# An output sum in a PSUM tile of its own, a new program order, single transfers, and weights split earlier, in a convolution with a gated feed-forward layer

## The chip, the cores and the metric

The kernel runs on one core of a Trainium2 chip. A core has a matrix engine (TensorE, PE in the profile, with its weight loads PEld), a vector engine (VectorE, DVE), an activation engine (ScalarE, ACT), GpSimd (POOL) and a queue that issues transfers (SyncE, SP). Each works through its own instructions in order and waits for the others by semaphores; 16 DMA engines carry the transfers. SBUF is the working memory, PSUM the accumulators that TensorE writes. The metric is the time of one execution in microseconds (us), as the median of several runs.

## What is computed

A causal convolution of 7 taps, one softmaxed set of taps for each of 8 heads, over x of shape (8, 4096, 192), then a feed-forward layer on the 32768 rows:

```python
w = softmax(weight)                      # (8, 7)
out[b, s, h, g] = sum_k w[h, k] * x_pad[b, s + k, h, g]
x = out.reshape(32768, 192)
xn = x / sqrt(mean(x * x) + 1e-6) * rms_g
g = xn @ w_gate                          # (192, 1536)
val = xn @ w_val
result = (silu(g) * val) @ w_out         # (1536, 192)
```

## The kernel before

**Tiles.** Rows go in pairs of two tiles of 512 (`T`), 1024 rows (`PT`) a pair, 32 pairs. The depth 192 is folded as 3 x 64, and gate and value products run side by side on the two halves of TensorE's rows (64 each). The hidden width 1536 is 12 blocks of 128, taken as 6 groups `j` of two blocks.

**The normal pair (2 to 31).** Both products are done with the seven-product scheme for a 2 x 2 block product. One factor is the pair's x in quarters, the other the weights. For exactness in the fast 32-bit format, each operand is split into three parts, so one product is 3 parts x 2 halves = 6 matmuls (line 936). A group `j` has 11 products, P1 to P7 and Q1 to Q4, into four blocks a, b, c, d, each a two-bank PSUM tile (one half gate, one half value): 66 products a pair. Between products the blocks are combined: `f1` copies a to b (ACT), `f3` copies c out (ACT), `f4` and `f5` add into c and d (DVE, line 1005). When a block is ready, `ga` to `gd` take the silu of its gate half (ACT, line 1011) and `ma` to `md` multiply its value half by that (DVE, line 1018); both give the PSUM tile back. The output product uses the scheme too: h sums `h1` to `h4` (POOL, line 988), then 42 output steps `o1.k` to `o7.k` of 12 matmuls (line 961) into three sums X, Y, Z, with `c1` (copy X to Y, ACT), `s7` and `c2` (copies of Z and X, ACT), `C21`, `C22` (DVE, line 1035) and the transposes `T11` to `T22` (DVE, line 976) into an output tile, which `st0` and `st1` store.

**PSUM.** Eight banks are four tiles of two banks (`duo`). A pool `pool4` hands them out in the order in which they came back. X and Z are the two halves of one of them (`"XZ"`), Y has one.

**Ahead of a pair.** For a later pair: `ld` (x loads by head), `cv0` to `cv6` (the taps; 0 on ACT, the others DVE line 437), `sq`, `red`, `pow`, `bc`, `mul` (the norm; `mul` is POOL line 516), `pl` (puts the result away in DRAM by heads), `ft` (fetches it back transposed into `rb`, line 662), `x1` to `x5` (sums of x quarters, line 862), and per group of operands `k`, `n`, `l`, `d` (the split; lines 835, 698, 843, 845).

**The weights.** `prepare` computes for each of 9 weight combinations the three split parts on POOL, DVE and ACT (lines 767 to 782) and stores them to DRAM (`wd`, line 786). It has 50 steps. From there a ring of 12 slots in SBUF is refilled while the pairs run (`ring_load`, line 804, 54 pieces a pair): a slot's next load is issued where its last product stands in the program, and SP waits there until TensorE has done it. `ring_start` issues the first 12.

**The order** is written out as words. `ORDER` is one normal pair, run for each pair, `FIRST` is pair 1, and `LINE` is the order of the products and output steps on TensorE. A word is an engine letter (V: DVE, A: ACT, G: POOL, S: SP), an operation and an index; `+` means that it works for a pair ahead, `-` for the pair before; `p3` issues the next three entries of `LINE`; `W` is one step of `prepare`, `R` is `ring_start`. Words of one engine run in the order written.

**The start.** Pair 0 and pair 1 use plain products (lines 1119 and 907) with unsplit weights. Pair 0's output phase (line 1160) is laid out on a time scale: every item is `put` at a place and emitted in the order of places; `base` is where the phase begins and its 96 steps are 37.5 units apart. Its sums leave PSUM by an ACT copy (line 1168) and a DVE addition (line 1172). Pair 1's products follow, 24 in thirds (72 steps, line 907), then its output steps. In `FIRST` the 50 `W` stand between pair 1's products, and `R` after them; the fetch of pair 2, `Sft.0+` to `Sft.2+`, comes after `R`. The taps of pair 2 run beside pair 0's output phase, cut in three pieces of 512 columns that accumulate in PSUM (`part_tap`, lines 453 and 461).

Of the kernel before, what the change touches and what calls it, by code (L numbers as in the profile page):

```python
# [11 lines left out]
F32 = mybir.dt.float32  # L12
# [8 lines left out]
def kernel(  # L21
# [28 lines left out]
    Q = 32  # L50
# [19 lines left out]
    HIGH = 0xFFFFF000  # L70
    PLAIN = tuple((j, c) for j in range(NP) for c in "abcd")
    ORDER = (
        "VT21- p2 Af1.0 p3 Af3.0 Spl.0+ Gh4.0- p1- Vf4.0 p1 Acv0++ p2 Aga.0 p1 p1- Spl.1+",
        "Gh4.3- Vma.0 Gh4.2- p1- Vf5.0 p1 Vcv1++ p1 Agc.0 Agb.0 Vmc.0 p1 Gh4.1- Gh4.4- Vmb.0",
        "Agd.0 Sst1- p2 Vmd.0 Spl.2+ Spl.3+ Af1.1 Sft.0+ p1 Vcv2++ Af3.1 p1 p2- Vf4.1 p1- p2",
        "Agc.1 p2 Vcv3++ VT12- Aga.1 Vmc.1 p1 Vf5.1 Gh1.0 p1 Gh3.0 Sft.2+ Agd.1 Vma.1 Sft.1+",
        "Vmd.1 p2 Af1.2 p3 Vcv4++ p1 Af3.2 Aga.2 Vf4.2 p2 Vma.2 Agb.1 p1 Vmb.1 Vf5.2 p2 Agc.2",
        "p1 Vmc.2 Agd.2 p2 Vmd.2 Vcv5++ Gh1.1 Af1.3 p1 Gx1+ Af3.3 p2 Vf4.3 p1 Agb.2 Vmb.2",
        "Gh1.2 Aga.3 Vma.3 p3 Agc.3 Vf5.3 Vmc.3 p2 Agd.3 Vmd.3 p1 Af1.4 p2 Gx3+ p1 Af3.4",
        "Vcv6++ Gx5+ Gh3.1 Agb.3 p1 Vf4.4 Gh3.2 p1 Aga.4 Vmb.3 p2 Agc.4 p1 Vma.4 Vf5.4 p1",  # L80
        "Sld.0+++ Vmc.4 Agb.4 p1 Agd.4 Gh1.3 p1 Vmb.4 p2 Vmd.4 Af1.5 Sld.1+++ p1 Af3.5 p2",
        "Gx2+ p1 Gx4+ p1 Gh1.4 Vk.3+ p1 Vd.3+ p1 Gh2.0 Vf4.5 An.3+ p1 Gh3.3 p2 Vl.3+ Aga.5 p1",
        "Vk.0+ p1 Gh3.4 Vma.5 Asq++ Agc.5 Gh2.1 Vf5.5 p1 Vd.0+ Vmc.5 An.0+ p1 Agd.5 Sld.2+++",
        "Ac1 Gh2.4 p1 Vmd.5 Gh2.3 Agb.5 p2 Sld.3+++ Gh2.2 p1 Vmb.5 Gh1.5 p1 Sld.4+++ Vred++",
        "p1 Sld.5+++ p1 Gh3.5 p4 Vl.0+ Sld.6+++ Gh2.5 As7 Vk.1+ p1 Vd.1+ p2 An.1+ Vl.1+ p2",
        "Vk.2+ Sst0- Gpow++ p2 Vl.2+ Vd.2+ p2 Ac2 p1 An.2+ p2 Vbc++ Vk.4+ p1 Sld.7+++ An.4+",
        "VT11 p1 VC21 Gh4.5 p1 Vd.4+ Vl.4+ p2 Gmul++ p1 VC22 VT22",
    )
# [1291 lines left out]
```

## Time and profile before

| | us |
|---|---|
| median of 3 runs | 2845.02 (2844.59 to 2846.81) |
| the profiled execution: its time | 2841.62 |
| the profiled execution: its span | 2839.7 |
| first matmul of pair 1 (line 907) | 134.7 |
| first matmul of pair 2 (line 936) | 274.5 |
| from pair 2 to pair 3 | 94.7 |
| from one pair to the next, pairs 3 to 30 | 84.1 to 87.6 |
| first matmul of pair 31 | 2747.3 |

Costs of single instructions, from the groups by line (mean ns, and how many):

```profile
L1005 DVE TENSOR_TENSOR ps<-ps,tt 128x1024 f32<-128x1024 f32 x360 | 443.5, 1232 | 216.8 <-PE ps L936 113.4
L1018 DVE TENSOR_TENSOR ht<-ps,tt 128x512 f32<-128x512 f32 x744 | 510.8, 688 | 255.0 <-ACT tt L1011 240.7
L437 DVE SCALAR_TENSOR_TENSOR y<-xh,tp,y 128x1536 f32<-128x1536 f32 x180 | 344.8, 1916 | 0.0
L862 POOL TENSOR_TENSOR tt<-xb 128x512 f32<-128x512 f32 x30 | 50.5, 1683 | 140.4 <-DMA xb<-xd 78.4
```

A row names the line, the engine, the operation, what it writes and reads, shape and count; behind the first bar the busy time and the mean duration in ns; behind the second the idle time of the engine just before such an instruction and what ended most of it. A busy engine is not by that on the path that sets the end; what counts is where TensorE, the busiest, stands and for whom.

### The profile page before, as it was taken

The page shows a single profiled execution, that of the slowest core. Times are in us where ns is not written, and L with a number is a line of the kernel's source. Part 1 is how long each engine was busy: PE and PEld are TensorE (multiplying, and loading weights), DVE is VectorE, ACT ScalarE, POOL GpSimd, SP SyncE. Part 2 cuts the span into 40 slices and gives each one's busy share as a digit, 9 for nine tenths or more (in the row PEclk, how much of TensorE's full clock was granted, in tenths as well). Part 3 has the DMA queues.
Part 4 walks back from the last instruction along what each step waited for, and adds up shares of the span by engine and source line. Part 5 has one row for each costly group of instructions (what it writes and reads, how often), then busy time and mean ns, then how long its engine had stood idle before and what let it go on. Part 6 is the DMA issues. An engine that isn't in the chain of part 4 may idle for free. (4 is left out here: it accounts for less than half of the span.)

```text
span 2839.7 us, 69721 instructions
## 1 busy us (share of the span) xinstructions
PE 2588.1 (91%) x28600; PEld 1871.5 (66%) x28600; DVE 2190.1 (77%) x2357; ACT 1138.0 (40%) x1559; POOL 1678.7 (59%) x1110
## 2 busy tenths in 40 slices
PE   9884999999999999999999999999999999999998
PEld 5633666666666666666666666666766666666676
DVE  8554778888877888787888778887878887877673
ACT  6331443343443343443343443344443434443332
POOL 0454556677546676556676556676556676556553
PEclk9997999999999999999999999999999999999999
DMA  6443766666766666766666766666766666766543
GB/s 132 75 139 92 194 185 170 153 161 170 207 179 169 152 159 173 205 182 171 153 161 169 205 182 177 153 159 170 202 187 177 160 152 169 194 188 181 146 135 90
DMA packets 741760, 467.14 MB, mean 165 GB/s; under 512 B 510914, under 2 KB 727746, under 8 KB 741442
## 3 DMA queue, kind: packets, MB, share of 16 engines
q1 hardware_dynamic: 737696, 461.76, 62.5%
q8 instruction: 227, 3.72, 0.6%
q10 hardware_dynamic: 3746, 0.92, 0.2%
q14 instruction: 91, 0.75, 0.1%
HBM read 402.35 MB, written 60.16 MB: 163 GB/s over the span
## 5 line engine op out<-in xcount | busy, mean ns | idle before, releaser
L936 PE MATMUL ps<-part,ring 64*128 64x512 f32 x11880 | 1517.6, 400 | 90.5 <-ACT ps L698 35.9
L936 PEld LDWEIGHTS ps<-part,ring 64*128 64x128 f32 x11880 | 1104.4, 185 | 462.0 <-ACT ps L698 91.2
L1011 ACT ACTIVATE tt<-ps 128x512 f32<-128x512 f32 x744 | 443.7, 597 | 825.1 <-PE ps L936 763.2
L988 POOL TENSOR_TENSOR hs<-ht 128x512 f32<-128x512 f32 x186 | 284.8, 1531 | 791.6 <-DVE ht L1018 768.6
L1018 DVE TENSOR_TENSOR ht<-ps,tt 128x512 f32<-128x512 f32 x744 | 510.8, 688 | 255.0 <-ACT tt L1011 240.7
L1005 DVE TENSOR_TENSOR ps<-ps,tt 128x1024 f32<-128x1024 f32 x360 | 443.5, 1232 | 216.8 <-PE ps L936 113.4
L988 POOL TENSOR_TENSOR ht<-ht 128x512 f32<-128x512 f32 x372 | 587.2, 1598 | 24.1 <-PE ps L961 19.3
L961 PE MATMUL ps<-ht,x 128*32 128x384 f32 (+2 forms) x6696 | 417.2, 382 | 85.7 <-ACT ps L698 59.7
L961 PE MATMUL ps<-ht,wo_sb 128*32 128x384 f32 (+2 forms) x6696 | 423.9, 383 | 0.8 <-DVE tt L1035 0.8
L961 PEld LDWEIGHTS ps<-ht,x 128*32 128x32 f32 x6696 | 286.9, 110 | 195.9 <-POOL ht L988 81.7
L961 PEld LDWEIGHTS ps<-ht,wo_sb 128*32 128x32 f32 x6696 | 290.6, 110 | 124.4 <-issue 36.3
L698 ACT COPY tt<-ps 128x384 f32<-128x384 f32 (+1 forms) x242 | 213.0, 880 | 362.2 <-PE ps L961 331.4
L437 DVE SCALAR_TENSOR_TENSOR y<-xh,tp,y 128x1536 f32<-128x1536 f32 x180 | 344.8, 1916 | 0.0
L988 POOL TENSOR_TENSOR ht<-hs,ht 128x512 f32<-128x512 f32 x186 | 296.0, 1612 | 51.8 <-PE ps L961 49.5
L698 ACT COPY ps<-ps 128x1024 f32<-128x1024 f32 (+1 forms) x211 | 194.5, 922 | 250.0 <-PE ps L936 194.8
L698 ACT CAST part<-tt 128x1024 fp32r<-128x1024 f32 (+1 forms) x150 | 144.1, 960 | 136.8 <-DVE tt L835 136.8
L835 DVE TENSOR_SCALAR tt<-tt 128x1024 uint32<-128x1024 uint32 (+1 forms) x60 | 140.9, 2348 | 61.5 <-ACT part L698 32.7
L961 PE MATMUL ps<-hs,x 128*32 128x128 f32 (+2 forms) x2232 | 139.6, 381 | 46.2 <-DVE tt L1035 46.2
L961 PEld LDWEIGHTS ps<-hs,x 128*32 128x32 f32 x2232 | 97.8, 110 | 80.8 <-DVE tt L1035 54.5
L862 POOL TENSOR_TENSOR tt<-xb 128x512 f32<-128x512 f32 x30 | 50.5, 1683 | 140.4 <-DMA xb<-xd 78.4
L843 DVE TENSOR_TENSOR part<-xb,tt 128x1024 fp32r<-128x1024 f32 x90 | 127.3, 1415 | 1.0
L845 DVE SCALAR_TENSOR_TENSOR part<-tt,xb 128x1024 fp32r<-128x1024 f32 x90 | 124.9, 1388 | 1.1
(128 smaller groups left out, 1517.5 us busy)
## 6 DMA issues: line engine op xcount, KB each, us to landing
ring<-wd SPq DMA_DIRECT2D x1620, 192.0 KB, 3.5
xb<-xd SPq DMA_DIRECT2D x186, 256.0 KB, 6.3
xd<-yn SPq DMA_DIRECT2D x244, 96.0 KB, 2.6
xh<-in_x_dram SPq DMA_DIRECT2D x192, 105.0 KB, 3.7
out_dram<-o_sb SPq DMA_DIRECT2D x122, 96.0 KB, 3.0
wd<-part SPq DMA_DIRECT2D x9, 1152.0 KB, 4.6
out_dram<-o_sb SPq DMA_DIRECT2D x60, 128.0 KB, 2.7
xh<-in_x_dram SPq DMA_DIRECT2D x56, 98.4 KB, 3.5
```

The lines of the kernel that those rows point to most:

```text
L437: nc.vector.scalar_tensor_tensor(out=y, in0=xk, scalar=w, in1=y, op0=ALU.mult, op1=ALU.add)
L698: nc.scalar.copy(out=dst, in_=src)
L835: nc.vector.tensor_scalar(out=high.bitcast(U32), in0=src.bitcast(U32), scalar1=HIGH, scalar2=None, op0=ALU.bitwise_and,)
L843: e.tensor_tensor(out=split_of(g, 1).bitcast(F32R), in0=src, in1=high, op=ALU.subtract)
L845: nc.vector.scalar_tensor_tensor(out=split_of(g, 2).bitcast(F32R), in0=high, scalar=1.0 + SPLIT, in1=src, op0=ALU.mult, op1=ALU.subtract,)
L862: engine[eng].tensor_tensor(out=dst, in0=a, in1=b, op=op)
L936: nc.tensor.matmul(out=self.both(j, c)[:, h, :], lhsT=left[HALF[h]], rhs=right[HALF[h]], start=(first and q == 0), stop=True, skip_group_c ...
L961: nc.tensor.matmul(out=self.acc(b)[i * Q : (i + 1) * Q, at : at + n], lhsT=left, rhs=cols, start=fresh, stop=True, skip_group_check=True, ...
L988: engine[eng].tensor_tensor(out=dst, in0=a, in1=b, op=op)
L1005: nc.vector.tensor_tensor(out=self.both(j, c), in0=self.both(j, "b"), in1=s5, op=ALU.add)
L1011: nc.scalar.activation(out=tt[:, t, :], in_=self.both(j, c)[:, 0, :], func=AF.Silu)
L1018: nc.vector.tensor_tensor(out=self.hv(j, "abcd".index(c)), in0=self.both(j, c)[:, 1, :], in1=tt[:, t, :], op=ALU.mult,)
```

## The change

- **PSUM tiles of the sums.** X, Y and Z each take a two-bank tile and use its first half. X and Z are opened at the first step of form 1 and of form 7; with `part` a tile that has been written only in part is taken first. Each is given back by itself: Z by `C21`, X by `T12`, Y by `T11`.
- **A new order**: `ORDER`, `FIRST` and `LINE` are new throughout. Among other things the x sums 1, 2 and 5 go from POOL (`Gx1`) to DVE (`Vx1`), `pow`, `bc` and `mul` move from the end of a pair to the beginning of the next one, and in `FIRST` the copy `Ac1` stands ahead of the split work.
- **Transfers one by one**: `pl`, `ft` and the stores `st` were issued two, two and five at a time by a word; each word now issues one transfer.
- **Weights**: the first 28 (`SOON`) of the 50 steps of `prepare` are put beside pair 0's output phase, 125 units apart from `base + 60` on; 22 `W` are left in `FIRST`, and `R` stands in the middle of pair 1's products.
- **Taps of pair 2**: `part_tap` goes; whole taps (`tap`) are put 210 units apart, the first on ACT.

```diff
+    SOON = 28
...
-        "VT21- p2 Af1.0 p3 Af3.0 Spl.0+ Gh4.0- p1- Vf4.0 p1 Acv0++ p2 Aga.0 p1 p1- Spl.1+",
...
+        "p3 Gh4.0- Gh4.3- Af1.0 Sld.7++ p2 p1- Gh4.5- p2- Af3.0 Gh4.4- Vf4.0 p1- p1 Agc.0 p2",
+        "p2- Vmc.0 Gpow+ p1 Vf5.0 Aga.0 p1 VT12- p1 Vma.0 p1 Agb.0 Vmb.0 Vbc+ p1 Af1.1 p2",
+        "Af3.1 Gmul+ p1 Aga.1 Spl.0+ Spl.1+ p1 Spl.2+ Sst0.4- Vf4.1 p2 Agd.0 Vmd.0 Vma.1",
+        "Acv0++ p3 Vf5.1 p1 Spl.3+ Agc.1 Spl.4+ p1 Spl.5+ Vcv1++ Agd.1 Agb.1 Vmc.1 Spl.6+",
+        "Vmd.1 p1 Spl.7+ p1 Af1.2 p1 Af3.2 p1 Sft.2+ Sft.0+ Vmb.1 p1 Vcv2++ Vf4.2 p1 Aga.2",
+        "Vma.2 Sst1.0- Sft.1+ Sft.3+ p1 Af1.3 Sst1.4- Sst1.1- p2 Vcv3++ Agc.2 Vmc.2 p1 Aga.3",
+        "Vma.3 p2 Gh1.1 Gh1.0 p1 Vf5.2 Af3.3 p2 Vf4.3 p3 Agb.2 Agd.2 Vmb.2 Vmd.2 Vf5.3 Agc.3",
+        "Sst1.3- Sft.4+ Sst1.2- Sst0.0- p4 Vmc.3 Gh3.0 Gh3.1 Gh1.2 Agd.3 Agb.3 p1 Vx1+ Vmd.3",
+        "Af1.4 p2 Af3.4 Vmb.3 Vcv4++ Gh1.3 p1 Vf4.4 p3 Aga.4 Gx3+ Vma.4 Vx2+ Gx4+ Gh3.2 p3",
+        "Agc.4 Vmc.4 p1 Vf5.4 p1 Vcv5++ Agb.4 Vmb.4 p3 Agd.4 Gh3.3 Vmd.4 Vk.3+ Vcv6++ Af3.5",
+        "p2 Af1.5 p1 Sld.0+++ Vf4.5 p2 Aga.5 Sld.1+++ p1 Vma.5 p2 Agc.5 Gh2.2 Gh2.0 Vf5.5",
+        "Gh2.1 Sld.2+++ p1 Gh1.4 Sld.3+++ Sld.4+++ Vmc.5 p1 Sld.5+++ Ac1 p1 Agd.5 Vmd.5 Agb.5",
+        "Sft.5+ Asq++ p3 Gh3.4 An.3+ p1 Gh2.3 Gh2.4 p2 Vmb.5 Vl.3+ Gh1.5 Vred++ p4 Gh3.5 p2",
+        "Gh2.5 As7 Vd.3+ p2 Vk.0+ p1 An.0+ Ac2 p2 Vd.0+ Vl.0+ Vk.1+ p3 An.1+ Gh4.2 Vl.1+ Vx5+",
+        "Vd.1+ Vk.2+ p4 Vl.2+ Vd.2+ Sst0.2- Sld.6+++ An.2+ Sst0.1- Sst0.3- p1 Vk.4+ p3 Vd.4+",
+        "VC21 Vl.4+ An.4+ p2 VT11 VC22 VT22 Gh4.1 VT21",
...
+        "Aga.5 Gh3.4 Vma.5 p3 Agb.5 Vmb.5 Vcv5++ p3 Agc.5 Vmc.5 p2 Agd.5 Vcv6++ Sft.0+ Sft.1+",
+        "Sft.2+ Sft.3+ Sft.4+ Sft.5+ p1 Vmd.5 p1 Gh2.0 Gh1.5 p1 Gh2.3 p1 Gh2.2 Sld.0+++ Gh3.5",
+        "p1 Gh2.1 p1 Gh2.4 Sld.1+++ Ac1 p1 Gh2.5 p1 Vx1+ p1 Gx3+ Vx2+ p1 Sld.2+++ Gx4+ p1",
+        "Sld.3+++ Vk.3+ p1 An.3+ Sld.4+++ Vl.3+ p1 Vd.3+ p1 Sld.5+++ Vk.0+ p1 Asq++ An.0+ p1",
...
+        "P1.0 Q1.0 P5.0 Q2.0 P6.0 P3.0 Q3.0 P7.0 P2.0 P4.0 P1.1 Q1.1 P5.1 Q2.1 P6.1 P2.1 Q4.0",
+        "P7.1 Q3.1 P1.2 Q1.2 P3.1 Q4.1 P4.1 P5.2 Q2.2 P6.2 P2.2 P1.3 Q1.3 Q3.2 P3.2 P2.3 P7.2",
+        "P5.3 Q2.3 P6.3 P4.2 Q4.2 P7.3 Q3.3 P3.3 P1.4 Q4.3 P4.3 Q1.4 P5.4 Q2.4 P6.4 P2.4 P1.5",
+        "Q1.5 P3.4 Q3.4 P7.4 P5.5 Q2.5 P4.4 Q4.4 o1.0 o1.3 o1.2 o1.1 P6.5 o1.4 P2.5 P7.5 Q3.5",
+        "P3.5 o1.5 Q4.5 P4.5 o6.0 o7.0 o7.1 o2.4 o6.2 o7.2 o6.1 o7.3 o7.4 o6.3 o7.5 o2.1 o2.2",
+        "o6.5 o6.4 o4.5 o4.1 o4.0 o4.4 o5.2 o5.1 o2.0 o5.3 o5.4 o2.3 o4.2 o4.3 o2.5 o5.5 o5.0",
+        "o3.0 o3.2 o3.1 o3.3 o3.4 o3.5",
...
-    def fetch(p, k):
...
+    def fetch(p, i):
+
+        k, rows = i // 2, (LOW, UPP)[i % 2]
+        nc.sync.dma_start(
+            out=rb[rows, k],
+            in_=scr[p][k * HP : (k + 1) * HP, :].rearrange("p (g t) -> p g t", t=T),
+        )
...
-        def open(self, name, full):
-            i = next((i for i in pool4 if i in full4 or not full))
+        def open(self, name, full, part=False):
+            used = [i for i in pool4 if i not in full4]
+            i = next(i for i in pool4 if i in full4) if full else (used * part + pool4)[0]
...
-            if b == "Y":
-                return duo[self.bk["Y"]][:, 0, :]
-            return duo[self.bk["XZ"]][:, "XZ".index(b), :]
+            return duo[self.bk[b]][:, 0, :]
...
-            if form in (1, 7) and "XZ" not in self.bk:
-                i = self.open("XZ", False)
-                full4.discard(i)
+            if form in (1, 7) and b not in self.bk:
+                full4.discard(self.open(b, False, True))
...
-                    self.give("XZ")
+                    self.give("Z", 2)
...
-                if b == "Y":
-                    self.give("Y", 2)
-                else:
-                    self.give("XZ")
+                self.give(b, 2)
...
-    def put_away(p, i):
-        if i == 0:
+    def put_away(p, h):
+        if h == 0:
...
-        for h in (2 * i, 2 * i + 1):
-            nc.sync.dma_start(out=to[h], in_=yn[p][h::H])
-        if i == H // 2 - 1:
-            yn.pop(p)
+        nc.sync.dma_start(out=to[h], in_=yn[p][h::H])
...
+    ready = itertools.chain(*[prepare(o) for o in range(NW)])
+    later(ready, *[base + 60 + 125 * i for i in range(SOON)])
...
-    for j in range(len(SIDE)):
-        put(c + 240 + 700 * (j // 2), functools.partial(part_tap, 2, 0, j))
-        for k in range(1, K):
-            at = c + 250 + 100 * k + 50 * j if j < 2 else c + 960 + 80 * k
-            put(at, functools.partial(part_tap, 2, k, j))
+    for k in range(K):
+        put(c + 40 + 210 * k, functools.partial(tap, 2, k, "A" if k == 0 else "V"))
```

`c` is `base + 200`. `leave`, which stores, takes the index of the one part of five that it stores.

## The prediction

> **What bounds the kernel now.** I read the page first: TensorE is busy for 91% of the span, no other engine for more than 77%. So the question is where PE idles.
>
> ```profile
> span 2839.7 us, 69721 instructions
> PE 2588.1 (91%) x28600; PEld 1871.5 (66%) x28600; DVE 2190.1 (77%) x2357; ACT 1138.0 (40%) x1559; POOL 1678.7 (59%) x1110
> 964.90:1050.50 85.60, 78.72 (x904) 58.00 (x900) 68.79 (x71) 34.78 (x46) 53.04 (x35) 1.00 0.67 172
> 1220.90:1305.00 84.10, 78.66 (x904) 57.27 (x901) 68.63 (x71) 34.76 (x46) 54.27 (x36) 1.00 0.67 176
> ```
>
> The last two lines are windows of one pair each (length, then PE, PEld, DVE, ACT, POOL, clock, DMA). Pairs 3 to 30 repeat every 84.9 us on average: PE works 78.7 and idles 6.2, DVE works 68.7. Pair 1 ends and pair 2 begins (first matmul of line 936) only at 274.5. The second view, the PE timeline of pair 10, shows each idle stretch in brackets:
>
> ```profile
> 985.57 3.02 PE L936 MATMUL ps<-part,ring 64*128 64x512 f32 x24 [0.47 <-DVE ps L1005]
> 989.04 8.48 PE L936 MATMUL ps<-part,ring 64*128 64x512 f32 x66 [0.45 <-ACT ps L698]
> 999.50 0.73 PE L936 MATMUL ps<-part,ring 64*128 64x512 f32 x4 [1.97 <-DMA ring<-wd]
> 1008.45 10.52 PE L936 MATMUL ps<-part,ring 64*128 64x512 f32 x84 [0.48 <-ACT ps L698]
> 1029.40 2.81 PE L961 MATMUL ps<-ht,x 128*32 128x384 f32 x48 [1.11 <-ACT ps L698]
> 1042.69 0.86 PE L961 MATMUL ps<-ht,x 128*32 128x384 f32 x12 [0.59 <-ACT tt L698]
> 1047.78 2.81 PE L961 MATMUL ps<-hs,x 128*32 128x384 f32 x48 [1.63 <-DVE tt L1035]
> ```
>
> Counting 6 matmuls to a product and 12 to an output step names the waiting step. The last three are o7.3 (into Z) behind `Ac1`, which copies X; o4.3 (Z) behind `Ac2`, which copies X; o5.4 (X) behind `VC21`, which reads Z. None needs that value: X and Z are two halves of one tile, and the wait is for the tile. Together 3.33 us. The first four, 3.37 us, belong to the gate products; the 1.97 is a weight slot that lands late while DMA is full:
>
> ```profile
> 985.00:990.00 5.00, 4.08 (x34) 3.41 (x34) 3.44 (x4) 2.59 (x4) 0.00 (x0) 1.00 1.03 290
> 990.00:995.00 5.00, 4.91 (x42) 3.49 (x40) 3.84 (x4) 1.73 (x3) 1.29 (x1) 1.00 1.07 252
> ```
>
> Third, the start: PE's timeline, SP's, and the waits between 214 and 284.
>
> ```profile
> 243.99 2.79 PE L961 MATMUL ps<-ht,x 128*32 128x384 f32 x24 [27.20 <-ACT ps L698]
> 255.05 1.50 PE L961 MATMUL ps<-ht,x 128*32 128x384 f32 x10 [8.27 <-POOL ht L988]
> ...
> 143.17 69.76 SPq L786 DMA_DIRECT2D wd<-part  x9
> ...
> 214.67 7.90 SPq L804 DMA_DIRECT2D ring<-wd  x12
> ...
> 223.61 4.20 SPq L662 DMA_DIRECT2D xb<-xd  x6
> ...
> ACT part L698 <- DVE tt L835: 39.8, 4, 27.0
> ...
> DVE tt L835 <- POOL tt L862: 25.4, 1, 25.4
> POOL tt L862 <- DMA xh<-in_x_dram: 21.7, 1, 21.7
> ```
>
> The nine weight pieces occupy SP until 212.9, the 12 ring loads come next, and pair 2's fetch (`Sft`, line 662) last, at 223.6. POOL's first x sum waits for it (the profile names an xh transfer of the same queue), DVE's `Vk.3` for POOL, ACT's `An.3` for DVE, and `Ac1` stands behind `An.3` on ACT. The tenth output step (o7.4, into Z) needs `Ac1` only by the shared tile, and PE stands 27.2 us.
>
> **The change part by part.**
>
> 1. *Start of pair 2.* Plain products end at 210.8 and pair 2 begins at 274.5: 63.7 us for 36 output steps, which at the steady rate (228 matmuls in 12.70, so 0.668 a step) are 24.0. New: the 28 early weight steps bring the ring start forward to the middle of pair 1's products, so nothing stands ahead of the fetch; `Ac1` precedes all split work on ACT; POOL's eight h sums (8 x 1.55 = 12.4 us) run while the fetch lands (first needed data at about 7.5 us after the products, from the queue's 250 GB/s and 1 MB plus issue). I take 2 us for steps that wait on h sums: 26. **Gain 37.7.**
> 2. *First steps of pair 2.* The rest of DVE's queue is then late: x1 at 7.5, and from it to `VC21` two x sums, k, l, d of five groups, the reduction and a wait for POOL's x3 come to 26 us, so P5.0, which takes Z's tile, comes at 34 where PE would be at 27.5: 6.6 lost, 7 with what follows. Before, this pair took 94.7, an excess of 9.8. **Gain 2.8.**
> 3. *Plain products.* 76.1 us now; 72 thirds at the undisturbed rate (60 matmuls in 13.37) are 63.2. The 12.9 lie beside 50 weight steps; 22 stay: 5.7. **Gain 7.2.**
> 4. *Pair 0's output phase* takes those 28 steps on DVE (0.72 and 1.05 a piece), ACT (0.84 twice) and POOL (1.97 once or twice). It already stands 5.18 us at 109.5 behind an ACT copy (1168) that is queued behind the square, which waits for DVE's taps. Six whole taps (6 x 1.81) replace 18 of 0.75, but weight steps stand among them and ACT's 782 waits for POOL: the square about 2.3 later. At the end POOL has some 21 us of work in 18, and the last copy, for which the first plain product waits, slips another 1.5. **Loss 3.8**; bounds: a gain of 5.2 (stand gone), a loss of 13 (all of the POOL work, 8 x 1.8, on the path, bar what covers it).
>
> Start in sum: 37.7 + 2.8 + 7.2 - 3.8 = **44 gained** (30 to 58).
>
> 5. *Own tiles.* The 3.33 us go: o6.0 truly follows `Ac1` but one product later, o5.2 follows `Ac2` by four steps, and `VC21` now precedes only P5.0. In their place four two-bank tiles have three sums in them: Z takes the tile that `Vmd.5` frees, X the one of `Vmb.4`, next pair's P5.0 that of Z, f1.0 that of Y.
> 6. *New order.* I went through it with 0.76 a product, 0.668 an output step, 0.3 from a product's end to the reader (Q4.3 to its activation), 0.6 an activation, 0.69 line 1018, 1.23 line 1005, 1.0 a copy, 1.81 a tap. PE is late at P7.1 behind f4.1 (0.4), P5.2 behind a tap and `Vmc.1` (0.3), P6.2 (0.3), P5.3 (0.3), P7.3 behind f4.3 (0.5), o1.0 behind tap 5 and `Vmb.4` (1.0), P7.5 behind k3, tap 6 and f4.5 (0.65), o7.0 behind `Vmd.5` (0.6), three small ones (0.6): 4.65. Without the longer hops this would be some 2.5; with one more tap's wait in each of two places 8.
> 7. *DVE* gets x1, x2, x5 from POOL: 3 x 0.69 = 2.1 us (half of line 843's 1.23 to 1.75 bounds one: 0.6 to 0.9). After `Vmb.5` its queue is full to the period's end: by the rows it has freed Z's tile 1.9 us before P5.0 asks and Y's 0.8 us before f1.0. That margin is all that covers these three; without it they cost 2.1 a pair. One row in the old tail shrinks, since `Gmul` moves away from `Vk.4`:
>
> ```profile
> 1043.62 3.11 DVE L835 TENSOR_SCALAR tt<-tt 128x512 uint32<-128x512 uint32 x1 [1.10 <-ACT part L698]
> ...
> 1043.44 3.00 POOL L516 TENSOR_TENSOR yn<-y,s 128x1536 f32<-128x1536 f32 x1
> ```
>
> The same operation took 0.69 at 239.8 beside no such POOL work.
> The Trainium skill, SBUF — State Buffer, section "Who interferes with whom", says that VectorE and GpSimd share a port pair as an exclusive lock, and that a VectorE tensor_tensor with two SBUF inputs contends with a GpSimd instruction that reads SBUF. This trace agrees for `Vk.4`; that x1, x2 and x5 would block so, no run here shows. It speaks against moving them.
>
> 8. *Transfers one by one.* No transfer is added; each costs its 0.6 us on SP as before. Before, 15 of them stood in 14 us ahead of the late slot. Now two of six fetches (0.5 MB, 2 us at 250 GB/s) and three of ten stores leave that stretch; but put-aways and four fetches still fall between 16 and 30 us of the pair, and a slot has 8.3 us from release to use (by counting the new list), as before. I take none left of the ring's wait (mean 1.0 a pair); 0 to 2. Three stores move behind `Sst` at 74 us, before T11 needs their buffer at 83.
>
> Steady: idle 4.65 instead of 6.2, so 1.6 x 29 pairs = **46 gained** (a loss of 50 to a gain of 107). The end of the kernel stays. Sum: 2839.7 - 44 - 46 = 2750 of span. The profiled execution took 2841.6, 3.4 under the median of 2845.0; against that median **2755**.
>
> **Rivals.** *A, nearly all handoffs covered:* idle 2.5, 3.7 x 29 = 107, in all 2845 - 151 = **2694**. For: three tile waits and the ring's wait vanish, and DVE's slack is 16 us a pair. Against: the list in 6. *B, the wait moves:* four tiles with three sums in them, `Vmd.5` and `Vmb.4` become what o7.0 and o1.0 wait for, idle stays 6.2: **2801**. For: DVE is nearly full at that place. Against: o-steps lie between in the new order. *C, slower: DVE becomes the bound.* If DVE keeps its 16.4 idle us a pair and adds 2.1, the period is 87.0: 2.1 x 29 = 61 lost, 44 gained, **2862**. It decides from a period of 86.4 on, at P5.0 and f1.0, when `VC21` and T11 come over 3 us late. Against: DVE's idle time is mostly waiting for PE.
> By the port rule each of the three would also wait for up to one POOL operation (1.28), and C would be 3.8 x 29 = 111 worse, 2973, an estimate.
>
> **Chances.** Forecast 0.45, A 0.23, B 0.2, C 0.1; 0.02 that the two parts cancel. Between A and B the time is continuous, so the range goes from 2685 to 2815. A median within 0.2% (6 us) cannot be told from no change: faster 0.88, same 0.02, slower 0.10.
>
> **What would show it.** Pair 2's first line-936 matmul at 228 to 238; the 27.2 gone; no wait of line 961 on `Ac1`/`Ac2`/1035 copies but on line 1018; DVE's k4 row at 0.7 to 1; period 83.3. Wrong: a stand of several us at the first P5 of each pair, x1 waiting for DMA on DVE with products queued behind it, or plain products starting past 148.

## The result, and the profile after

The changed kernel takes **2909.8 us** (median of 4, 2902.4 to 2914.1) beside 2844.8 for the kernel before in the same session: a ratio of **1.0225**, 95% interval 1.0203 to 1.0246. It is slower by 2.2%; the forecast was 2755 and its range ended at 2815. The profiled execution took 2902.4 us. Its page, and the window of pair 10 (from its first gate product to the next pair's; columns as before: length, then busy PE, PEld, DVE, ACT, POOL, granted clock, DMA share, GB/s):

```profile
span 2900.3 us, 69736 instructions
PE 2633.9 (91%) x28600; PEld 1888.1 (65%) x28600; DVE 2236.1 (77%) x2435; ACT 1151.8 (40%) x1557; POOL 1623.1 (56%) x1020
947.60:1035.80 88.20, 79.97 (x902) 57.87 (x900) 70.66 (x75) 35.09 (x47) 50.04 (x32) 0.98 0.63 167
```

The mean period of the steady pairs went from 84.9 to 88.2 us. Two things grew for the same 28600 matmuls: PE's idle time, and PE's busy time (2588.1 to 2633.9 us), so that the same work ran slower. A stand is idle time of PE ahead of an instruction. PE's timeline of pair 10 has these stretches that begin after a stand (start, length, work, stand in brackets):

```profile
949.58 0.50 PE L905 MATMUL ps<-part,ring 64*128 64x512 f32 x2 [0.65 <-DVE part L813]
951.79 0.50 PE L905 MATMUL ps<-part,ring 64*128 64x512 f32 x2 [1.71 <-DVE part L815]
953.55 3.79 PE L905 MATMUL ps<-part,ring 64*128 64x512 f32 x18 [1.25 <-DVE tt L1003]
970.48 5.06 PE L905 MATMUL ps<-part,ring 64*128 64x512 f32 x42 [0.28 <-DVE ps L973]
975.87 11.27 PE L905 MATMUL ps<-part,ring 64*128 64x512 f32 x90 [0.33 <-DVE ht L986]
987.75 2.33 PE L905 MATMUL ps<-part,ring 64*128 64x512 f32 x18 [0.61 <-DVE ps L973]
991.66 12.89 PE L905 MATMUL ps<-part,ring 64*128 64x512 f32 x102 [1.57 <-DMA ring<-wd]
1006.23 2.81 PE L929 MATMUL ps<-ht,wo_sb 128*32 128x384 f32 x48 [1.68 <-DVE ht L986]
```

None of the old waits for a shared tile is left. The first three lines stand at the **join**, the first 6 us of a pair: Q1.0 waits for parts 2 and 3 of group 2's operand (`Vl.2`, `Vd.2`), then P5.0 for Z's tile, which `VC21` (line 1003) must read first. Together 3.61 us; in the kernel before no pair has a stand there. Four of the other lines wait for VectorE, as the forecast's hand list has it; the 1.57 is a weight slot of the ring. What VectorE does before the next join (pair 11 begins at 1035.9), and what GpSimd does at that time:

```profile
1025.87 2.31 DVE L813 TENSOR_TENSOR part<-xb,tt 128x1024 fp32r<-128x1024 f32 x1
1028.28 1.58 DVE L805 TENSOR_SCALAR tt<-xb 128x1024 uint32<-128x1024 uint32 x1
1029.89 1.23 DVE L813 TENSOR_TENSOR part<-xb,tt 128x1024 fp32r<-128x1024 f32 x1
1031.04 1.77 DVE L832 TENSOR_TENSOR xb<-xb 128x512 f32<-128x512 f32 x1
...
1035.66 2.19 DVE L813 TENSOR_TENSOR part<-xb,tt 128x1024 fp32r<-128x1024 f32 x1
1037.78 2.29 DVE L815 SCALAR_TENSOR_TENSOR part<-tt,xb 128x1024 fp32r<-128x1024 f32 x1
...
1041.27 0.55 DVE L1003 TENSOR_TENSOR tt<-ps,tt 128x384 f32<-128x384 f32 x1
```

```profile
1025.03 4.28 POOL L956 TENSOR_TENSOR ht<-ht 128x512 f32<-128x512 f32 x2 [0.89 <-PE ps L929]
...
1032.83 6.16 POOL L956 TENSOR_TENSOR ht<-ht 128x512 f32<-128x512 f32 x3 [0.57 <-PE ps L929]
```

No row of VectorE has a bracket: from 1017.6 to 1044.6 it is never idle. The same line 813 operation takes 1.23 us at 1029.89 and 2.31 or 2.19 beside GpSimd's h sums of line 956 (`Gh4`, two and three in a row here). Last, the clock around the stands of that join, in windows cut where the clock of this trace can change (see the last section):

```profile
1035.21:1038.63 3.42, 2.54 (x26) 1.17 (x16) 3.38 (x3) 1.05 (x1) 3.42 (x2) 1.00 0.17 46
1038.63:1042.04 3.41, 0.67 (x4) 0.35 (x6) 3.24 (x5) 0.62 (x1) 3.24 (x3) 1.00 0.03 12
1042.04:1045.45 3.41, 3.41 (x18) 2.51 (x18) 2.54 (x8) 1.73 (x2) 0.53 (x3) 0.50 0.23 60
```

PE is busy 0.67 of the 3.41 us ahead of 1042.04, and then the granted clock (third figure from the end) is 0.50 for 3.41 us. What that costs stands in the rows of pair 10 above, where the clock falls to 0.50 at 953.29: 18 product matmuls take 3.79 us at 953.55 and 2.33 at 987.75.

The start did gain, if less than forecast. PE's timeline:

```profile
117.10 3.85 PE L1117 MATMUL ps<-wo_sb,ht 64*128 64x192 f32 x24 [11.28 <-ACT o_sb L1125]
125.44 10.63 PE L1117 MATMUL ps<-wo_sb,ht 64*128 64x192 f32 x96 [4.50 <-ACT o_sb L1125]
...
150.32 64.16 PE L876 MATMUL ps<-xb,part 64*128 64x512 f32 x288 [0.72 <-DVE o_sb L1129]
...
233.20 4.41 PE L929 MATMUL ps<-ht,x 128*32 128x384 f32 x48 [3.31 <-ACT tt L670]
```

Pair 0's output phase now stands 19.6 us, and the plain products begin at 150.3 instead of 134.7. They then take 64.2 us instead of 76.1 (one stretch, no stand), the stand of 27.2 us is gone, and pair 2 begins at 245.7 instead of 274.5.

### The profile page after: what moved, and what is told of

Read it like the earlier page. It is cut to its first block, busy times and chain, and to the rows that moved or that the text cites. A ratio compares the mean times of both kernels' runs of the same rounds, so it can differ in the third digit from the quotient of the medians.

```text
span 2900.3 us, 69736 instructions
## 1 busy us (share of the span) xinstructions
PE 2633.9 (91%) x28600; PEld 1888.1 (65%) x28600; DVE 2236.1 (77%) x2435; ACT 1151.8 (40%) x1557; POOL 1623.1 (56%) x1020
## 4 chain that ended last, share of the span: by engine, by line
PE 38%; DVE 37%; DMA 9%; issue 6%; ACT 5%; POOL 4%; SPq 1%; DVEq 0%; ACTq 0%; POOLq 0%
PE ps L905 26%; PE ps L929 9%; DVE part L815 6%; DVE y L438 6%; DMA ring<-wd 6%; DVE part L813 6%; DVE ht L986 5%; DVE tt L805 5%; ACT tt L979 3%; DVE ps L973 3%; POOL yn L489 3%; PE ps L876 2%; DMA xd<-yn 2%; DVE xb L832 2%; DVE s L461 2%
## 5 line engine op out<-in xcount | busy, mean ns | idle before, releaser
L905 PE MATMUL ps<-part,ring 64*128 64x512 f32 x11880 | 1564.7, 410 | 195.9 <-DVE part L815 51.3
L905 PEld LDWEIGHTS ps<-part,ring 64*128 64x128 f32 x11880 | 1137.6, 191 | 575.3 <-DVE ht L986 92.2
L956 POOL TENSOR_TENSOR ht<-ht 128x512 f32<-128x512 f32 x372 | 678.2, 1840 | 109.1 <-PE ps L929 101.6
L956 POOL TENSOR_TENSOR hs<-ht 128x512 f32<-128x512 f32 x186 | 351.5, 1895 | 549.7 <-DVE ht L986 549.2
L929 PE MATMUL ps<-ht,wo_sb 128*32 128x384 f32 (+2 forms) x6696 | 445.9, 389 | 30.5 <-DVE ht L986 29.8
L489 POOL TENSOR_TENSOR yn<-y,s 128x1536 f32<-128x1536 f32 x31 | 92.8, 2993 | 390.7 <-issue 376.0
L956 POOL TENSOR_TENSOR ht<-hs,ht 128x512 f32<-128x512 f32 x186 | 270.5, 1476 | 68.1 <-PE ps L929 65.8
L813 DVE TENSOR_TENSOR part<-xb,tt 128x1024 fp32r<-128x1024 f32 x90 | 171.7, 1907 | 2.0
L805 DVE TENSOR_SCALAR tt<-xb 128x1024 uint32<-128x1024 uint32 x90 | 140.6, 1563 | 11.8 <-POOL xb L832 1.2
L929 PE MATMUL ps<-hs,x 128*32 128x384 f32 (+2 forms) x2232 | 147.8, 379 | 0.8 <-ACT tt L670 0.8
```

The lines of the kernel that those rows point to most:

```text
L489: e.tensor_tensor(out=yn[p].rearrange("p a t -> p t a"), in0=y, in1=ss[:].rearrange("p (t o) -> p t o", o=1).to_broadcast([P, TB, GS]), op ...
L805: nc.vector.tensor_scalar(out=high.bitcast(U32), in0=src.bitcast(U32), scalar1=HIGH, scalar2=None, op0=ALU.bitwise_and,)
L813: e.tensor_tensor(out=split_of(g, 1).bitcast(F32R), in0=src, in1=high, op=ALU.subtract)
L905: nc.tensor.matmul(out=self.both(j, c)[:, h, :], lhsT=left[HALF[h]], rhs=right[HALF[h]], start=(first and q == 0), stop=True, skip_group_c ...
L929: nc.tensor.matmul(out=self.acc(b)[i * Q : (i + 1) * Q, at : at + n], lhsT=left, rhs=cols, start=fresh, stop=True, skip_group_check=True, ...
L956: engine[eng].tensor_tensor(out=dst, in0=a, in1=b, op=op)
```

## Experiments

All single runs stand beside 2839 to 2843 us for the kernel before. The theory: **VectorE's queue at the end of a pair is too long, made so by contention with GpSimd's h sums, and the join's stands also lower the clock.** Rival 1: the three x sums moved to VectorE are the load. Rival 2: the own tiles cost, as they come free later.

**1. The h sums `h4` left out**, here and in `FIRST`: the output product then reads values without these sums.

```diff
-"p3 Gh4.0- Gh4.3- Af1.0 ... Gh4.5- p2- Af3.0 Gh4.4- Vf4.0 ..."
+"p3 Af1.0 ... p2- Af3.0 Vf4.0 ..."
...
-"... Vk.1+ p3 An.1+ Gh4.2 Vl.1+ Vx5+ Vd.1+ Vk.2+ ... VT22 Gh4.1 VT21"
+"... Vk.1+ p3 An.1+ Vl.1+ Vx5+ Vd.1+ Vk.2+ ... VT22 VT21"
```

> The changed kernel without its 186 h4 sums on POOL (form 3 of the output product then reads the unsummed values). Theory: POOL's h4 sums run beside DVE's split work at the end of a pair and stretch it (lines 813, 815 and 805 at 2.2, 2.3 and 1.6 us instead of 1.2, 1.2 and 0.7), so that the parts of Q1.0's operand and Z's tile come 3.6 us late at the start of the next pair. Expected: those rows fall to about 1.3, 1.3 and 0.9 at the end of a pair, the waits at P1.0 to P5.0 shrink from 3.6 to under 1 us, the period from 88.2 to 83 to 85. Rival 1 (DVE simply has too much to do by the three x sums): rows and period change by under 1 us. Rival 2 (the tiles of the sums): the wait for Z's tile stays at 1.2 us or more.

Measured: **2728.0**, a period (from one pair's start to the next) of 82.0, no stand at the join, a clock of 0.989. Of the 6.2 us gained a pair, 3.2 are idle time of PE and 2.9 busy time. VectorE's groups of the same operations (count, then busy and mean ns) in the changed kernel, and without `Gh4`:

```profile
L813 DVE TENSOR_TENSOR part<-xb,tt 128x1024 fp32r<-128x1024 f32 x90 | 171.7, 1907 | 2.0
L832 DVE TENSOR_TENSOR xb<-xb 128x512 f32<-128x512 f32 x30 | 51.0, 1699 | 0.0
```

```profile
L811 DVE TENSOR_TENSOR part<-xb,tt 128x1024 fp32r<-128x1024 f32 x90 | 110.2, 1225 | 2.0
L830 DVE TENSOR_TENSOR xb<-xb 128x512 f32<-128x512 f32 x30 | 20.8, 695 | 0.0
```

The second group is x5. With unstretched rows the new order does what the forecast said it would, and somewhat better. So the order of the steps is not at fault by itself; the durations are. One reservation: the run also takes the h sums' own time from GpSimd.

**2. The three x sums given back to GpSimd**, here and in `FIRST`.

```diff
-"Vx1+ ... Vx2+ ... Vx5+"
+"Gx1+ ... Gx2+ ... Gx5+"
```

> The changed kernel with the x sums 1, 2 and 5 back on POOL, at the same places of the order. Rival 1 (the three sums on DVE are what is too much): DVE's queue is shorter by 2 to 3 us a pair and the period falls from 88.2 to about 85.5. Theory (it is the split work beside POOL's sums): only x5 leaves DVE's last stretch, 0.7 to 1.8 us of it, and POOL has one more sum there, so the waits at the join fall from 3.6 to 2 to 3.5 us and the period by 0 to 2.

Measured: **2935.5**, period 89.3; the stands at the join are still there. Worse, not better: GpSimd then has five h sums in one row up to the join, and the group of VectorE's long rows is longer still (timeline of GpSimd, then VectorE's group):

```profile
1132.29 10.10 POOL L955 TENSOR_TENSOR ht<-ht 128x512 f32<-128x512 f32 x5
```

```profile
L812 DVE TENSOR_TENSOR part<-xb,tt 128x1024 fp32r<-128x1024 f32 x90 | 198.8, 2209 | 2.0
```

The mean is 2209 ns where it was 1907. Rival 1 falls: the moved sums help. So did my own expectation of a small gain: by the longer mean, a later GpSimd prolongs the overlap.

**3. Group 1's split moved** behind `Vf4.0` of the new pair (and out of `FIRST`), so that groups 2 and 4, `VC21` and T11 come earlier in VectorE's queue.

```diff
-"... Vf4.0 p1- p1 Agc.0 ..."   "... Vl.0+ Vk.1+ p3 An.1+ Gh4.2 Vl.1+ Vx5+ Vd.1+ Vk.2+ ..."
+"... Vf4.0 Vk.1 An.1 Vl.1 Vd.1 p1- p1 Agc.0 ..."   "... Vl.0+ Vx5+ Vk.2+ p3 An.2+ Gh4.2 ..."
```

> The changed kernel with DVE's split of operand group 1, which no product needs before P2.0 (10 us into the pair), moved from the end of a pair behind f4.0 of the pair itself, and group 2, which Q1.0 needs, made before it; C21 one place forward. Theory: DVE reaches group 2 and C21 some 5 us earlier, the 3.6 us of waits at the join vanish, with them the fall of the granted clock there (0.66 at 1042 to 1047), and the period falls from 88.2 to 83.5 to 85; at most 1.5 us come back at f5.0 and P4.0, which stand behind the moved split. Rival 1 (DVE has too much to do in all): the wait only moves to P3.0, P2.0 or P4.0, the period stays above 87.

Measured: **2792.6**, period 84.6; the join's 3.6 us become 0.21 (tile of Z) and 1.21 (f1.0 behind T11):

```profile
919.04 1.65 PE L904 MATMUL ps<-part,ring 64*128 64x512 f32 x12 [0.21 <-DVE tt L1002]
921.91 0.96 PE L904 MATMUL ps<-part,ring 64*128 64x512 f32 x6 [1.21 <-ACT ps L669]
```

Hardly anything was made cheaper here (VectorE is busy for 2216.4 us in all instead of 2236.1); work was moved off the tail. That is the wait for VectorE shown directly, and the kernel is now faster than before.

**4. X and Z in one tile again, the rest of the change kept.**

```diff
-            return duo[self.bk[b]][:, 0, :]
+            if b == "Y":
+                return duo[self.bk["Y"]][:, 0, :]
+            return duo[self.bk["XZ"]][:, "XZ".index(b), :]
...
```

> The changed kernel with X and Z again in the two halves of one PSUM tile, everything else as changed. Theory (own tiles cost little, the end of DVE's queue costs the time): the tile waits of the old kernel come back (up to 3.3 us a pair at the copies of X, of Z, and at C21), P5.0 no longer waits for C21, so the period goes to 88 to 91. Rival 2 (three sums in four tiles are what costs): P5.0 and o7.0 get their tiles earlier and the period falls below 87.

Measured: **3013.0**, period 91.9 (88 to 91 expected), and no stand at the join. The shared tile brings a stand of its own in the output steps:

```profile
891.85 2.79 PE L931 MATMUL ps<-hs,x 128*32 128x384 f32 x24 [6.58 <-DVE tt L1005]
```

An output step into the other half now waits for `VC21`, which is late. Own tiles are worth 3.7 us a pair in the new order; rival 2 falls.

**5. P1.0 issued four times**, to fill the stand ahead of Q1.0 with work.

```diff
-            for q in range(3):
+            for q in [0, 1, 2] * (4 if w == "P1" and j == 0 else 1):
```

> The changed kernel with the first plain product of each group 0 (P1.0) issued four times over, each time from the start of its sum, so that the result is the same and 9 more matmuls of about 0.23 us, some 2.1 us of TensorE work, stand in each pair right ahead of Q1.0, where TensorE stood 0.65 + 1.71 us in the changed kernel for parts 2 and 3. Theory (the stands at the join also lower the granted clock for some microseconds after them, to 0.66 in the window after 1042 us, and this costs about 2 us of a pair): the added work lies inside the wait for the parts, that wait falls from 2.4 to under 0.5 us, the clock after it stays above 0.9, and a pair takes 86.0 to 87.8 instead of 88.2, 2850 to 2900 us in all, although more is computed. Rival (the waits alone cost, the clock nothing): the added work takes the place of the wait and a pair stays at 88.0 to 88.6, 2900 to 2915.

Measured: 2896.4, period 88.0, mean clock 0.982 instead of 0.963. (The expectation says 9 more matmuls; the loop issues 18, which at the list's 0.76 us for a product's 6 are 2.3 us.) The kernel with more work is the faster one, but one run decides little here: the time lies in the theory's range, the period in the rival's. What decides is the split of a pair. Idle time fell by 0.8 us (7.63 to 6.79), and busy time rose by only 0.6 (80.55 to 81.18) where 2.3 us of work came in, so some 1.7 us of slow clock went. The trace has it directly: the clock is at 0.50 for 2.6 us a pair instead of 6.0. It did not go everywhere: P5.0's stand of 1.25 remained, and in 20 of the 28 pairs the clock still fell. The clock is a second cost of the stands, of at least 1.7 us a pair.

**6. No early weight steps**: all 50 among pair 1's plain products.

```diff
-    SOON = 28
+    SOON = 0
...
```

> The changed kernel with no weight step in pair 0's output phase: all 50 stand among pair 1's plain products. Theory (the 28 early weight steps, in ScalarE's and GpSimd's queues ahead of pair 0's output copies and behind VectorE's whole-length taps, make TensorE stand 19.6 us in that phase): pair 1's plain products begin at 134 to 140 instead of 150.3 and take 70 to 76 instead of 64.2, pair 2 begins at 240 to 249 instead of 245.7, the steady pairs stay at 88.2; in all within 6 us of 2902. Rival (the whole-length taps of pair 2 put in pair 0's phase hold VectorE, weights or not): plain products still begin at 146 to 151, and pair 2 later than 252.

Measured: 2925.2. The stands in pair 0's output phase fall from 19.6 to 9.5 us:

```profile
117.01 10.47 PE L1118 MATMUL ps<-wo_sb,ht 64*128 64x192 f32 x96 [8.07 <-ACT o_sb L1126]
...
138.32 43.17 PE L877 MATMUL ps<-xb,part 64*128 64x512 f32 x192 [0.72 <-DVE o_sb L1130]
```

The plain products begin at 138.3, take 75.7, and pair 2 begins at 249.3. Splitting the weights early moves some 11 us from one phase into the one ahead of it; it gains almost nothing in sum. One stand of 8.07 us stays without weight steps: the whole taps ahead of the square (before it was 5.18). The total was expected within 6 us of 2902 and is 23 above it: the steady period was 88.8 where 88.2 was expected, for which I have no cause.

**7. The kernel before with own tiles alone**, o7.0 and o7.1 behind P4.5.

```diff
-"... o1.4 o7.0 P7.5 Q3.5 P3.5 o7.1 o1.5 Q4.5 P4.5 o7.3 ..."
+"... o1.4 P7.5 Q3.5 P3.5 o1.5 Q4.5 P4.5 o7.0 o7.1 o7.3 ..."
...
```

> The kernel before with one part of the change alone: each output sum X, Y, Z in a PSUM tile of its own, in the old program order, with o7.0 and o7.1 moved behind P4.5 because Z opens later; taps, transfers and early weights as before. Theory (own tiles are good by themselves, and what made the changed kernel slow is the new order's join): the three waits for the shared tile, 3.33 us a pair, mostly go, a pair takes 82.0 to 83.8 instead of 84.9, in all 2755 to 2810. Rival (an own tile is only as free as the copies that empty it, so that the waits come back as waits for C21 and T11): a pair within 0.6 of 84.9, in all 2825 to 2865.

Measured: **2830.2**, period 84.3: a gain of 0.6 a pair instead of the theory's 1.1 to 2.9, at the edge of the rival's range. In the pair shown the three tile waits went, but what stood behind o7.0 and o7.1 comes up to 1.3 us earlier and now waits:

```profile
1027.82 1.65 PE L935 MATMUL ps<-part,ring 64*128 64x512 f32 x12 [0.57 <-DVE ps L1003]
1031.37 4.11 PE L959 MATMUL ps<-ht,x 128*32 128x384 f32 x72 [1.89 <-DVE ht L1016]
```

Of 3.33 us removed 2.46 came back, most likely because o7.0 and o7.1 had filled the time in which these operands were made.

**8. Group 4's split behind `VC21` and T11 as well** (on top of 3).

```diff
-"... Vk.4+ p3 Vd.4+ VC21 Vl.4+ An.4+ p2 VT11 VC22 ..."
+"... p3 VC21 p1 VT11 Vk.4+ Vd.4+ An.4+ Vl.4+ p1 VC22 ..."
```

> The changed kernel with group 1's split moved behind f4.0 of the new pair and with C21 and T11 taken ahead of group 4's split on VectorE. Theory (the join's waits are VectorE's queue: parts 2 and 3, C21, T11 come too late in it): against the earlier run with group 1's split moved alone (a pair of 84.6, waits of 0.21 and 1.21 us left at the join) the wait behind T11 goes as well, the waits at the join are under 0.5 us together, the granted clock is above 0.985, a pair takes 82.5 to 83.8, in all 2725 to 2770. Rival (the wait only moves to group 4's split, which Q4.0 then waits for, or to GpSimd's h sums): a pair of 84.2 to 85.5, 2780 to 2815.

Measured: **2792.1**, period 84.3. The join, the first 6 us, has no stand at all, as the theory said (one of 0.66 us for f4.0 comes behind it), yet the time is the rival's. What is left is in the gate phase, and pairs come in two kinds. Two pairs of this kernel as windows, and the stands in the middle of the first:

```profile
924.20:1008.90 84.70, 79.33 (x902) 59.08 (x900) 69.39 (x74) 34.94 (x46) 50.89 (x32) 0.98 0.67 174
1179.10:1261.80 82.70, 77.61 (x904) 57.23 (x902) 69.48 (x76) 35.24 (x47) 50.55 (x33) 1.00 0.68 179
```

```profile
959.75 1.66 PE L904 MATMUL ps<-part,ring 64*128 64x512 f32 x12 [0.62 <-DVE ps L972]
961.77 0.96 PE L904 MATMUL ps<-part,ring 64*128 64x512 f32 x6 [0.36 <-DMA ring<-wd]
964.36 13.85 PE L904 MATMUL ps<-part,ring 64*128 64x512 f32 x102 [1.62 <-DMA ring<-wd]
```

In the first pair 2.60 us of stands fall within 5.2 us, the clock then drops to 0.57 (mean of 964.2 to 968.2) and the pair's busy time is 1.7 us more. In the second the stands at that place are 0.62 and 1.58, 2.2 in all, and the clock stays at 1.00. What tells the two apart is where the stands lie: the clock of this trace changes only at marks 3.41 us apart. Windows from mark to mark, two of the first pair and two of the second:

```profile
961.30:964.71 3.41, 1.43 (x12) 0.85 (x12) 2.53 (x3) 0.60 (x1) 0.94 (x1) 1.00 1.06 277
964.71:968.13 3.42, 3.42 (x20) 3.20 (x18) 0.42 (x2) 0.60 (x1) 0.00 (x0) 0.50 0.99 331
...
1213.89:1217.30 3.41, 2.52 (x20) 1.61 (x18) 2.83 (x4) 0.94 (x3) 1.29 (x1) 1.00 1.08 247
1217.30:1220.71 3.41, 2.09 (x18) 2.03 (x20) 1.61 (x3) 0.72 (x2) 0.00 (x0) 1.00 1.10 367
```

In the first pair 1.98 us of idle time lie between two marks, and the clock is 0.50 for the 3.4 us behind the second. In the second pair a mark cuts the stands into 0.89 and 1.32 us, and no fall comes. Of the 28 pairs from 3 to 30, the 10 without a fall take 82.0 to 83.4 us and the 18 with one 84.0 to 86.9. So the ring's wait, which the forecast had put at none, costs twice in most pairs: as idle time, and by the clock.

**9. The six output stores moved behind that place** (on top of 8).

```diff
-"... Sst1.0- Sft.1+ Sft.3+ p1 Af1.3 Sst1.4- Sst1.1- ... Sst1.3- Sft.4+ Sst1.2- Sst0.0- p4 Vmc.3 ..."
+"... Sft.1+ Sft.3+ p1 Af1.3 ... Sft.4+ p4 Vmc.3 ... Vmd.3 Sst1.0- Sst1.4- Sst1.1- Sst1.3- Sst1.2- Sst0.0- ..."
```

> The kernel with the rebuilt tail (groups 1 and 4 moved, 2792) with one more move: all six output stores of the pair before that stood in SyncE's queue in the middle of the gate phase (o_sb to out_dram, behind the xb fetches) now come after the stretch in which ring loads are late, right behind the first x sum. Theory (the waits of 1.6 to 2.8 us for a ring slot come from SyncE's queue: 17 put-aways, fetches and stores of 0.35 to 0.6 us each stand among the ring loads between 942 and 961 us; and with such a wait the idle time of TensorE within 6 us passes about 2.6 us and the granted clock falls for 2 to 4 us, which makes the pairs of 84 to 85 out of those of 82.6): three stores fewer ahead of the late slot take about 1.3 us from each wait, the mean ring wait falls from 2.05 to under 1.0 us a pair, hardly any pair shows a fall of the clock, and a pair takes 82.3 to 83.3 instead of 84.4, in all 2725 to 2765. Rival (the 16 DMA engines are full there at a share of 1.0, and an earlier issue only lands as late): ring wait within 0.4 of 2.05, a pair of 84.0 to 84.8, 2780 to 2800.

Measured: 2776.4, period 84.0, ring wait 1.83 a pair instead of 2.05 (the same kernel has 1.58 in 12), and still 17 of 28 pairs with a fall of the clock. The theory fails (and its 2.6 us within 6 is not the rule of the clock, as 8 shows). Of the 16 us gained, 8 are an earlier start of pair 2 (247.9 instead of 255.8), and that is chance: pair 0's output phase itself began 7.5 us earlier. Fewer issues of SyncE ahead of the slot thus bought little. That the ring wait stays fits the rival: the 16 DMA engines were at shares of 0.99 to 1.11 in that stretch of the version of 8.

**10. Two fetches moved behind it too.**

```diff
-"... Vma.2 Sft.1+ Sft.3+ p1 Af1.3 ... Agc.3 Sft.4+ ..."
+"... Vma.2 p1 Af1.3 ... Agc.3 Sft.1+ Sft.3+ Sft.4+ ..."
```

> As the kernel with the stores late, and in addition two of the four fetches (xb from xd, 256 KB each) that stand ahead of the late ring slot moved behind it, next to the fifth. Theory: the ring wait goes as a whole (under 0.3 us a pair), a pair takes 81.8 to 82.8, in all 2710 to 2745. Rival (x1 and the POOL x sums then wait for the fetches on VectorE and GpSimd, with products queued behind them): the ring wait goes but new waits for VectorE of 1 us or more stand in the gate phase, a pair of 83.0 to 85.0.

Measured: **2958.4**, period 90.1. The ring wait falls to 0.1 us a pair in the mean, and x1 on VectorE takes its place, with a stand of PE of 5 to 9 us in every pair:

```profile
930.56 0.69 DVE L831 TENSOR_TENSOR tt<-xb 128x512 f32<-128x512 f32 x1 [9.42 <-DMA xb<-xd]
```

```profile
932.99 9.90 PE L904 MATMUL ps<-part,ring 64*128 64x512 f32 x66 [9.10 <-ACT ps L669]
```

This is the rival, far above its price. It suggests that the fetches press on the ring loads, though pairs that are 6 us longer also give these more time. VectorE's in-order queue does not let them come later unless x1 moves too; that was not tried.

**11. Tap 5 behind `Vmd.4`** (on top of 9).

```diff
-"... Vf5.4 p1 Vcv5++ Agb.4 Vmb.4 p3 Agd.4 Gh3.3 Vmd.4 Vk.3+ ..."
+"... Vf5.4 p1 Agb.4 Vmb.4 p3 Agd.4 Gh3.3 Vmd.4 Vcv5++ Vk.3+ ..."
```

> The kernel with the rebuilt tail and the late stores (2776 in one run) with one word moved: tap 5 of the next pair's convolution (1.81 us on VectorE) stands behind Vmb.4 and Vmd.4 instead of ahead of Vmb.4. Theory (what the hand list of the prediction named: o1.0 waits 0.8 to 1.0 us for Vmb.4, which stands behind that tap): the wait of o1.0 on VectorE falls from 0.9 to under 0.2 us, nothing else waits for the tap, a pair takes 83.0 to 83.6 instead of 84.0; in all 2740 to 2772, faster than the kernel before by 2.6 to 3.7%. Rival (VectorE only meets the delay later, at P7.5 or o7.0, which need f4.5 and Vmd.5 behind tap 6): the wait goes over to these, a pair 83.8 to 84.4, 2770 to 2790.

Measured in five rounds: 2805.6 (2801.6 to 2820.5), a ratio to the kernel before of 0.9867 (0.9846 to 0.9889); the period of its profile, which is of the slowest round, is 85.5. The stand of o1.0 remains and another is added:

```profile
982.82 2.81 PE L928 MATMUL ps<-ht,wo_sb 128*32 128x384 f32 x48 [0.77 <-DVE ht L985]
989.76 2.36 PE L904 MATMUL ps<-part,ring 64*128 64x512 f32 x18 [1.55 <-DVE ps L972]
```

The rival's mechanism holds, above its price (2770 to 2790): P7.5 now waits for f4.5 behind the tap. The first line says that o1.0's wait was never mainly the tap (0.79 us a pair in the mean, 1.01 in the version of 9); my hand list named the wrong reason for a right number.

**12. The version of 9, timed.**

> The version with the rebuilt tail (groups 1 and 4 moved) and the late stores once more, now timed in five rounds against the kernel before, because single runs of these kernels differ by some 10 us. Theory: the gain seen in one run (2776.4 against 2842.6) is no accident of the run: a median of 2768 to 2792, 1.8 to 2.6% faster than the kernel before, pairs in two kinds, about 82.5 us without and 84.8 with a fall of the granted clock. Rival (as for the version with tap 5 moved, whose rounds lay between 2802 and 2821): a median above 2795.

Measured: **2774.6** (2768.7 to 2776.2), a ratio to the kernel before of **0.9735** (0.9713 to 0.9757). It beats both kernels: 2.6% faster than the one, 4.6% faster by the medians than the changed one. Its profile has the two kinds of pairs as expected: 13 without a fall of the clock, 82.5 us in the mean, and 15 with one, 84.8. All that differs from the changed kernel is the order of VectorE's words around a pair's end and six stores, and the single run of 3 had most of the gain.

## Why the prediction was wrong

The direction was wrong, by 151 us of span (2750 forecast, 2900.3 measured). The steady pairs account for 142 of them: 88.2 instead of 83.3, 29 times. Of the 4.9 us, 3.0 are idle time (7.63 a pair where 4.65 were listed) and 1.9 are busy time of the same matmuls (80.55 where 78.65 were taken; the kernel before has 78.8) at a mean clock of 0.963 instead of 0.988. The start accounts for 5 and the end for the rest. Two of the forecast's own signs of being wrong came: the stand ahead of the first P5 of a pair, and plain products that start past 148.

- **The step that failed is 7, the margin on VectorE**: "by the rows it has freed Z's tile 1.9 us before P5.0 asks and Y's 0.8 us before f1.0". `VC21` in fact came 1.25 us after P5.0 asked, with PE already 2.4 us late. In the rows from 1021 to 1040 seven were 0.9 to 1.1 us longer than the same operation in experiment 1, 6.8 us in all (five are shown above, the others are line 805 at 1023.14, 1.55 us, and at 1034.04, 1.58 us): this is what used up the margin. The forecast took the short durations for all of them and named only one long row of the old tail. Experiment 1 shows the tail with short rows, and there the period is 82.0. The kernel before has the same stretching (its line 843 averages 1.41 us), but no stand at its join.
- **The forecast also missed a deadline.** Q1.0 needs `Vl.2` and `Vd.2` within the first 2 us of a pair. Only P5.0 and f1.0 were tested; the first 2.36 us of the join are Q1.0's.
- **Rival C had the place and the mechanism** (P5.0, with `VC21` over 3 us late, VectorE the bound there) at a chance of 0.1 and a price of 2862. The price was too small, since it counted three more sums and not the longer rows, nor a slower clock after the stands. Its reason against (VectorE's idle time is mostly waiting for PE) is true of the pair as a whole, 70.7 busy of 88.2, and says nothing of a stretch of 27 us in which it is never idle.
- **On the port rule** of the Trainium skill (SBUF — State Buffer, "Who interferes with whom"), the trace agrees where two inputs lie in SBUF: 1.23 us becomes 2.19 to 2.31, 0.69 becomes 1.77, and GpSimd's sums go from 1.28 to 2.05. But I weighed the rule only against the three sums that the change moved, where it priced C at 2973. It applied to every such row of the tail, moved or not, and experiment 2 shows that moving the three was right. The row that it was checked on, `Vk.4`, has one tensor and a constant, and so did not show the case of two inputs.
- **Step 6, the hand list: right in sum, by luck.** It gave 4.65 us a pair; pair 10 has 4.47 in the five rows outside the join. But 1.57 of that is a ring wait, which the list did not hold, so its own places come to 2.9. And it gave o1.0 the tap as a reason, which 11 refutes.
- **Step 5, own tiles: right.** The waits went, and 4 prices the tiles at 3.7 us a pair in the new order. In the old order (7) most of it comes back.
- **Step 8 was mis-sized, within its bounds**: none was taken as left of the ring's wait, and 1.6 us a pair stand in the mean (the bound was 2; before it was 1.0).
- **Step 4 was mis-sized, and out of its bounds**: 15.6 us lost instead of 3.8. One row for each engine shows why, in the order in which they wait for each other (VectorE, GpSimd, ScalarE):

```profile
109.06 8.36 DVE L438 SCALAR_TENSOR_TENSOR y<-xh,tp,y 128x1536 f32<-128x1536 f32 x3
```

```profile
109.22 3.31 POOL L750 TENSOR_TENSOR part<-part 128x768 f32<-128x768 f32 x1 [5.22 <-DVE part L746]
```

```profile
115.83 0.84 ACT L744 ACTIVATE part<-part 128x768 f32<-128x768 f32 x1 [2.43 <-POOL part L737]
```

  Three taps take 8.36 us instead of 5.4 and each weight operation on GpSimd 3.31 instead of 1.81, at the same time (line 750 at 109.22, and line 737, for which ScalarE waits, at 112.49); PE's copy stands behind line 744 on ScalarE. Again the sum was made from durations measured alone.
- **Steps 1 to 3**: pair 2's 36 output steps took 31.2 us (26 forecast), the plain products 64.2 (69), and pair 2 itself 88.1, no more than a later pair, where 7 us extra were forecast. All three gained, 54 us together by their own rows, and step 4 took 15.6 back: 39 of the 44 forecast. That the start came within 5 us of its forecast is luck: step 4 missed by 12 and step 1 by 5, and steps 2 and 3 gained 12 more than forecast.

Open: why the ring's wait differs from pair to pair, and why the pairs of experiment 6 take 88.8, was not settled.

## What to carry to other kernels

Before work is moved to an engine, or an order is packed tighter, list what the engine does in the last stretch before each consumer's deadline and use for each row the duration that it has beside the work that will then run next to it; an average load of 80% hides a tail that is full. When a wait is removed, test every operation that then comes earlier against all its inputs, and take the new waits as likely as the gain. And price a group of short stands by what follows as well: here some 2 us of idle time between two marks of the clock cost another 1.7 us of slow matmuls.

## What the runs showed of the hardware

- **The granted clock falls without any long stand.** In every trace of this case it is 1.00 or 0.50 and nothing between, and it changes only at marks 3.41 us apart. What decides is the idle time of PE from one mark to the next, whether in one stand or in several (changed kernel: 0.65, 1.71 and 1.25 us; experiment 8: 0.62, 0.36 and 1.62). The 14 traces hold 9858 such stretches at a clock of 1.00 between the starts of pairs 2 and 31: none of the 9269 with less than 1.2 us idle was followed by a fall, all 193 with 2.0 us or more were, and 93 of the 396 between. A fall in these pairs lasts 3.4 us, or 6.8 or more. The Trainium skill (TensorE: Matmul & The Clock Gate, "HAM oscillation — how this bites in real kernels") warns of idle gaps over about 3.4 us; by these rows some 2 us in pieces are enough. Its section "What's actually happening" speaks of a free-running activity window of about that length, and the marks of these traces fit it.
- **GpSimd and VectorE lengthen each other's operations by 0.8 to 1.5 us** when both read two tensors from SBUF (VectorE 1.23 to 2.31 and 0.69 to 1.77, GpSimd 1.28 to 2.05 and 1.81 to 3.31), and VectorE's by 0.9 where VectorE's operation has one tensor and a constant (line 805: 1.58 us instead of 0.69).
